# A fused linear-attention and MLP kernel: the hand-written order of its work, the priorities of its kinds of instruction and two buffer counts are changed

## The chip, the cores and the metric

The kernel runs on one core of a Trainium2 chip. The metric is the device time in microseconds (us) of one execution, the median of three runs. TensorE is called PE here, its weight loads PEld, VectorE DVE, ScalarE ACT, GpSimd POOL; SyncE (SP) issues all DMAs.

## The reference

```python
B, H, S, D = 4, 8, 768, 48
mag = sqrt(a_re**2 + a_im**2); scale = minimum(mag, 0.999) / (mag + 1e-6)
ar, ai = a_re * scale, a_im * scale
for t in range(S):                       # a complex decay per channel, one state per head
    S_re, S_im = ar*S_re - ai*S_im + outer(k[t], v[t]), ar*S_im + ai*S_re
    y[t] = q[t] @ S_re
x = y as (B*S, H*D) = (3072, 384)
h = x @ w_in                             # (3072, 2048)
out = (h - tanh(h)) @ w_out              # (3072, 384)
```

The inputs a, q, k, v are float32 and the weights reach the kernel as 64-bit words.

## The kernel before

The recurrence is computed in 6 chunks of 128 time steps (`NC`), for 4 batches; a *unit* u is one chunk of one batch (24 of them), a *pair* g is two units of one chunk (12 of them). Every product that needs more than 16 bits is made of three passes over a high and a low float16 half (`PASS`). The first four units (`PLAIN`) use float32 matmuls instead.

The work of a pair is cut into steps that a plan names by letters:

- `F`, `B`, `b`, `C`, `D`, `E`: the gates of a pair (L236 to L328). B and b take logarithms and exponentials of the decay, C the arctangent and the running sums of the angles (two matmuls with `tri` per batch, `cumsum`, L215) after loading the `carry` of the chunk before, D the sines (`g_trig`), E the running sums of the logarithms and their exponentials (`g_ep`, `g_en`), and `hd` by a trip through DRAM. `F0` and `F1` are the first pair's.
- `p`: `products(u)` (L371), in three pieces: q times its gates, split in two halves and transposed by a DMA into `qT` (L405); k the same into `kT`; then v and the load of the unit two further on.
- `a`: `attention(u)` (L428), in five pieces: S for four heads (12 matmuls of `kT` with `qT`, L450), masked on DVE into `af`; S for the other four heads; QU, the old state's part (L467, 24 matmuls of `qT` with `z16`); AV (L474), which ends with y scaled into `x16` and transposed by a DMA into `xT` (L479) and a square for a later check (`junk`, L480); Z, the new state. A sixth call does nothing.
- `i`, `o`: `decode` (L172) of two of the 16 tiles of w_in or w_out into two float16 halves, only before and during pair 0; `q` loads q, k, v of a unit; `w`: a square of decoded weights for the check (L198).

The main loop (L604 to L620) runs over the 12 pairs, and in each over 8 values of fp: `head(g, fp)` (L507) makes 18 matmuls of `xT` with w_in into `h`, then tanh on ACT and a subtraction on DVE (`mt`); after every second one `split` (L528) makes the two halves of g (`mg`); `tail` (L537) makes 12 matmuls into `o`, running up to LAG behind. Between them the steps of the plan are written down: a plan entry `5:a2` means: at step 5 (of 16, two for each fp; the even one after the head, the odd one after the tail), the next piece of attention of unit 2g+2. So while pair g goes through the MLP, the attention of pair g+1 is made. START holds for the time before pair 0, FIRST for pair 0, SECOND for pair 1, CYCLE for all others.

This is the order in the program. The order on each engine is laid down once, when the kernel is built, by a list scheduler with its own estimates of durations: of the instructions that it takes to be ready, the one that stands earliest in the program goes first, after its place has been moved forward by the offset of its kind (`At`, L93): OFFSET for pairs from 2 on, EARLY before that (L606). A negative offset moves it back. On the chip each engine works through its list in order and waits where an operand or a buffer is late. Activations that need a table are chained in program order by hand (`chained`, L335). DMAs are all in SP's list.

PSUM: three buffers for `h` (`ps_h`), three for `att` (`ps_a`: S, y, the running sums and the state's update share them), one pair for `o`. BUFS counts the buffers of some SBUF tiles; those without a count have one (`a_raw`, `g_t1`, `junk`).

Of the kernel before, what the change touches and what calls it, by code (L numbers as in the profile page):

```python
# [18 lines left out]
B, H, S, D = 4, 8, 768, 48  # L19
# [23 lines left out]
BUFS = {"io": 3, "wtmp": 4, "mt": 2, "mg": 4, "qkf": 2, "xT": 2, "a16": 3, "af": 2, "x16": 1, "qT": 4, "kT": 2, "vv": 2, "z16": 2}  # L43
LAG = 3
START = (
    "F0 F1 i0 B1 b1 i1 o3 q0 q1 p0 p0 i2 p1 p0 a0 p1 p1 o1 a1 o0 a0 a1 i5 E1 a1 i4 a1 a0 o4 C1 i3 i7 D1 a0 p2 "
).split()
FIRST = tuple((int(i), x) for i, x in (y.split(":") for y in (
    "0:p3 0:a0 0:a1 1:p2 1:i6 1:p2 2:a2 3:o7 3:o5 4:a2 4:a2 4:p3 5:B2 5:o2 5:b2 6:p3 7:a2 7:C2 9:a3 9:a2 9:a3 10:a3 11:D2 12:B3 12:b3 13:a3 14:E2 14:p4 14:p4 14:p4 15:o6 15:p5 15:a3 "
).split()))  # L50
SECOND = tuple((int(i), x) for i, x in (y.split(":") for y in (
    "0:p2 0:p2 1:a1 1:p2 2:a2 2:a2 3:C2 4:p2 4:p3 6:D2 7:p2 7:a2 7:a0 7:p3 7:a1 8:a2 9:a3 9:p2 9:w0 10:a3 10:a2 11:a3 11:E2 11:p4 11:B3 11:b3 13:a3 13:a3 14:w1 "
).split()))
CYCLE = tuple((int(i), x) for i, x in (y.split(":") for y in (
    "0:p2 0:p2 0:p3 0:w0 2:p2 2:p3 4:p3 4:a2 5:C2 5:a2 5:D2 7:a2 7:a2 8:a3 9:a3 9:a3 10:a2 10:a3 10:a3 10:B3 11:E2 11:b3 11:a2 15:w1 "
).split()))
OFFSET = {"gate": 2000, "gatep": -300, "prod": 0, "prodp": 400, "qkhi": 400, "vhi": -100, "vlo": -100, "zhi": -300, "zlo": -300, "S": 30, "af": -300, "ahi": 0, "alo": -2000, "qu": 0, "y": 0, "xf": 100, "kv": 30, "z": 30, "guard": -2000, "h": 0, "tanh": -30, "mt": 400, "ghi": 2000, "glo": 4000, "o": 0, "out": -30, "dec": -100, "dechi": 400, "declo": 4000, "table": 0, "cum": 0, "load": 2000}
EARLY = {"gate": 200, "gatep": 100, "prod": 0, "prodp": 2000, "qkhi": -30, "vhi": 0, "vlo": 700, "zhi": 4000, "zlo": -300, "S": 100, "af": 400, "ahi": -30, "alo": -100, "qu": 100, "y": 400, "xf": 0, "kv": 700, "z": 200, "guard": -30, "h": 0, "tanh": 30, "mt": -30, "ghi": 100, "glo": 4000, "o": 0, "out": -700, "dec": 0, "dechi": 1000, "declo": 400, "table": -300, "cum": 100, "load": 0}
# [28 lines left out]
def tile_fast(ctx: ExitStack, tc: tile.TileContext, flag, a_in, qkv_in, win_in, wout_in, sq_c, vec_c, lim_c, out):  # L87
# [84 lines left out]
    def decode(fp, kind):  # L172
        src = (win_in, wout_in)[kind]
        raw = sb.tile([P, 4, DM], F32, name="io", bufs=BUFS["io"]).rearrange("p x n -> p (x n)").bitcast(I32).rearrange("p (n two) -> p n two", two=2)
        for j in range(2):
# [650 lines left out]
```

## Time and profile before

| what | value |
|---|---|
| time before, median of 3 runs | 584.81 us (583.1 to 588.11) |
| the profiled execution | 584.0 us |
| its span, first to last instruction | 582.2 us |
| busy: PE, PEld, DVE, ACT | 506.6, 386.9, 459.2, 452.5 us |
| mean granted TensorE clock | 0.967 |

The difference between the profiled execution and its span, 1.8 us, lies around the program. A stretch of the span is read by setting its length against the busy time of each engine in it: an engine that is busy throughout sets its length. Matmuls are pipelined, so that the row of one overlaps the start of the next by up to 0.2 us.

### The profile page before, as it was taken

The numbers are of one execution on the slowest core, as the hardware profiler recorded it, in microseconds if no ns is written. First come the engines' busy times: TensorE is split into PE (matmuls) and PEld (weight loads), VectorE is DVE, ScalarE is ACT, GpSimd is POOL, SyncE is SP. The second block draws the span as 40 slices with busy tenths as digits, with TensorE's granted clock in tenths as the row PEclk, the third lists the DMA queues.
The fourth block names the chain that finished last, engine by engine and source line by source line (L and its number), as shares of the span: only waits on it lengthen the run. The fifth ranks groups of instructions, "written<-read, shape, count | busy, mean of one in ns | idle before, by whom it ended". The sixth has DMA issues, their size and how long they took to land.

```text
span 582.2 us, 12341 instructions
## 1 busy us (share of the span) xinstructions
PE 506.6 (87%) x5058; PEld 386.9 (66%) x5058; DVE 459.2 (79%) x674; ACT 452.5 (78%) x784; POOL 1.9 (0%) x8
## 2 busy tenths in 40 slices
PE   2564989978999889889889989889889899999995
PEld 0343867756678668668668668668668577787772
DVE  4999998876998978878978977977987977953321
ACT  7988899978888968968968968968978969643441
POOL 1000000000000000000000000000000000000000
PEclk9886899988999999999999999999999899999998
DMA  8778632096473573583763572762672641720001
GB/s 259 237 254 224 212 126 78 16 186 137 79 163 98 101 141 97 101 142 97 101 140 97 108 137 94 109 142 87 120 155 65 138 103 49 139 69 15 1 28 33
DMA packets 133899, 68.07 MB, mean 117 GB/s; under 512 B 119982, under 2 KB 123694, under 8 KB 133836
## 3 DMA queue, kind: packets, MB, share of 16 engines
q1 hardware_dynamic: 133836, 67.21, 49.9%
q8 instruction: 41, 0.67, 0.5%
q14 instruction: 22, 0.18, 0.1%
HBM read 36.73 MB, written 4.78 MB: 71 GB/s over the span
## 4 chain that ended last, share of the span: by engine, by line
PE 47%; DVE 17%; ACT 14%; DMA 13%; issue 6%; SPq 1%; ACTq 0%; DVEq 0%
PE h L515 16%; PE o L546 16%; PE att L102 11%; DMA kT<-k 6%; DMA qT<-q 3%; DVE g_t L102 3%; DVE a_raw L102 2%; ACT a_raw L102 2%; DVE qkv_raw L390 2%; PE att L467 2%; DMA g_t<-carry 2%; DVE qkf L393 2%; ACT L346 2%; DVE k L119 2%; ACT g_t L102 1%
## 5 line engine op out<-in xcount | busy, mean ns | idle before, releaser
L515 PE MATMUL h<-xT,w 128*128 128x256 f16 x1728 | 212.8, 275 | 18.6 <-DMA xT<-x 16.5
L546 PE MATMUL o<-w,mg 128*128 128x384 f16 x1152 | 207.8, 327 | 1.4 <-DVE mg L102 1.3
L515 PEld LDWEIGHTS <-w 128*128 128x128 f16 x1728 | 168.0, 99 | 48.8 <-issue 11.9
L546 PEld LDWEIGHTS <-mg 128*128 128x128 f16 x1152 | 111.6, 98 | 66.7 <-DVE mg L102 2.0
L102 ACT ACTIVATE mt<-h 128x512 f32<-128x512 f32 x96 | 56.4, 590 | 56.8 <-PE h L515 56.5
L102 DVE SCALAR_TENSOR_TENSOR mt<-h,mt 128x512 f32<-128x512 f32 x96 | 65.3, 685 | 38.9 <-ACT mt L102 38.9
L102 DVE SCALAR_TENSOR_TENSOR mg<-mt,mg 128x1024 f16<-128x1024 f32 x48 | 58.7, 1222 | 21.8 <-ACT mg L102 21.4
L102 PE MATMUL att<-qT,kT 96*128 96x128 f16 (+1 forms) x544 | 46.9, 236 | 16.9 <-DMA kT<-k 14.1
L102 ACT ACTIVATE mg<-mt 128x1024 f16<-128x1024 f32 x48 | 50.5, 1052 | 7.7 <-DVE mt L102 7.5
L102 ACT ACTIVATE a_raw<-a_raw 128x768 f32<-128x768 f32 (+2 forms) x49 | 39.2, 802 | 6.3 <-DVE a_raw L102 6.1
L102 PEld LDWEIGHTS <-kT 96*128 96x128 f16 x480 | 30.9, 101 | 18.6 <-DMA kT<-k 17.1
L393 DVE TENSOR_TENSOR qkf<-qkv_raw,g_trig 128x768 f32<-128x768 f32 x44 | 40.9, 949 | 0.0
L102 DVE TENSOR_TENSOR af<-att,sqc 128x512 f32<-128x512 f32 x40 | 27.4, 688 | 14.9 <-PE att L102 14.7
L346 ACT ACT_TABLE_LOAD x24 | 30.8, 1283 | 0.4
L102 DVE TENSOR_TENSOR a<-af,a 128x512 f16<-128x512 f32 x40 | 26.8, 684 | 2.9 <-ACT a L112 2.9
L102 ACT ACTIVATE q<-qkf 128x768 f16<-128x768 f32 x20 | 16.9, 844 | 10.4 <-DMA qT<-q 10.4
L112 ACT ACTIVATE a<-af 128x512 f16<-128x512 f32 x36 | 21.7, 626 | 2.9 <-DVE af L102 2.9
L102 DVE SCALAR_TENSOR_TENSOR g_t<-g_t,a_raw 128x768 f32<-128x768 f32 (+1 forms) x26 | 23.0, 887 | 0.9 <-ACT a_raw L102 0.9
L102 ACT ACTIVATE g_t<-att 128x384 f32<-128x384 f32 x24 | 10.7, 485 | 15.7 <-PE att L221 9.9
L102 ACT ACTIVATE g_trig<-g_t 128x768 f32<-128x768 f32 (+1 forms) x26 | 20.3, 782 | 0.3 <-DVE g_t L102 0.2
L102 ACT ACT_TABLE_LOAD x15 | 19.2, 1283 | 1.0 <-PEq L819 0.8
L119 DVE TENSOR_TENSOR q<-qkf,q 128x768 f16<-128x768 f32 x20 | 19.0, 950 | 1.2 <-ACT q L102 1.2
(96 smaller groups left out, 674.4 us busy)
## 6 DMA issues: line engine op xcount, KB each, us to landing
qkv_raw<-in_qkv SPq DMA_DIRECT2D x24, 576.0 KB
a_raw<-in_a SPq DMA_DIRECT2D x22, 384.0 KB
io<-in_win SPq DMA_DIRECT2D x16, 384.0 KB
io<-in_wout SPq DMA_DIRECT2D x16, 384.0 KB
out_dram<-io SPq DMA_DIRECT2D x24, 192.0 KB
a_raw<-in_a SPq DMA_DIRECT2D x4, 192.0 KB
xT<-x SPq DMA_TRANSPOSE x24
hd<-hscr SPq DMA_DIRECT2D x20, 3.0 KB
```

The costliest lines, as they stand in the source:

```text
L102: return f(*a, **k)
L112: A(kind).activation(out=out, in_=in_, func=AF.Copy, scale=scale)
L119: by_name[ENGINE[which]](kind).tensor_tensor(**k)
L346: chained(A("table").preload_act_table_set(name))
L390: V("prod").scalar_tensor_tensor(out=x, in0=vw(e), scalar=E_MAX, in1=x, op0=ALU.min, op1=ALU.mult)
L393: V("prod").tensor_tensor(out=f, in0=x[:, :, None].broadcast_to([P, H, 2, D]), in1=tg[:, :, sl].rearrange("p r (h d) -> p h r d", d=D), op ...
L467: T("qu").matmul(y_ps[:, h * D:(h + 1) * D], lhsT=qT[0:K, qp * H + h], rhs=z16[0:K, zp, h * D:(h + 1) * D], start=(h == 0 and n == 0), sto ...
L515: T("h").matmul(h_ps[:, j].rearrange("p (two t) -> p two t", two=2), lhsT=wi[ft][:, wp, kt * P:(kt + 1) * P], rhs=xT[:, :, xp, kt, :], sta ...
L546: T("o").matmul(o_ps[:, tt, :DM], lhsT=gg[:, gp, fp % 2, j * 256 + tt * P:j * 256 + (tt + 1) * P], rhs=wo[ft][:, wp], start=(ft == 0 and n ...
```

## The change

Two buffer counts, the three plans and START, and offsets of some kinds are other numbers or another order; no function changes. `qux` and `prodp` are not used by any function. In CYCLE the order of the pieces of attention of unit 2g+3 goes from steps 8, 9, 9, 10, 10 to 7, 9, 10, 10, 10, and the second product of that unit from step 2 to 1; C2 and D2 stand together; w0 and w1 go from steps 0 and 15 to 3 and 13.

```diff
--- before.py
+++ after.py
@@ -40,23 +40,23 @@
 STEP = [round((s + 1) * DEC / math.log(2)) for s in range(P)]
 PLAIN = 4
 HALF = [n // 2 for n in STEP]
-BUFS = {"io": 3, "wtmp": 4, "mt": 2, "mg": 4, "qkf": 2, "xT": 2, "a16": 3, "af": 2, "x16": 1, "qT": 4, "kT": 2, "vv": 2, "z16": 2}
+BUFS = {"io": 3, "wtmp": 4, "mt": 2, "mg": 3, "qkf": 2, "xT": 2, "a16": 3, "af": 2, "x16": 1, "qT": 3, "kT": 2, "vv": 2, "z16": 2}
 LAG = 3
 START = (
-    "F0 F1 i0 B1 b1 i1 o3 q0 q1 p0 p0 i2 p1 p0 a0 p1 p1 o1 a1 o0 a0 a1 i5 E1 a1 i4 a1 a0 o4 C1 i3 i7 D1 a0 p2 "
+    "F0 i0 o3 F1 B1 i1 q0 q1 p0 p0 i2 p1 p0 a0 p1 b1 o0 p1 a1 o1 a0 a1 i5 E1 a1 i4 a1 i3 a0 o4 C1 i7 a0 D1 p2 "
 ).split()
 FIRST = tuple((int(i), x) for i, x in (y.split(":") for y in (
-    "0:p3 0:a0 0:a1 1:p2 1:i6 1:p2 2:a2 3:o7 3:o5 4:a2 4:a2 4:p3 5:B2 5:o2 5:b2 6:p3 7:a2 7:C2 9:a3 9:a2 9:a3 10:a3 11:D2 12:B3 12:b3 13:a3 14:E2 14:p4 14:p4 14:p4 15:o6 15:p5 15:a3 "
+    "0:p3 0:a0 0:a1 1:p2 1:i6 1:p2 2:a2 3:o7 3:a2 3:o5 3:a2 4:p3 4:B2 5:b2 6:p3 7:a2 7:C2 7:o2 9:a3 9:a2 9:a3 10:D2 10:a3 12:B3 12:b3 13:a3 13:a3 14:E2 14:p4 14:p4 15:o6 15:p5 "
 ).split()))
 SECOND = tuple((int(i), x) for i, x in (y.split(":") for y in (
-    "0:p2 0:p2 1:a1 1:p2 2:a2 2:a2 3:C2 4:p2 4:p3 6:D2 7:p2 7:a2 7:a0 7:p3 7:a1 8:a2 9:a3 9:p2 9:w0 10:a3 10:a2 11:a3 11:E2 11:p4 11:B3 11:b3 13:a3 13:a3 14:w1 "
+    "0:p2 0:p2 0:a2 1:p2 2:p2 3:a2 3:C2 4:p2 5:a1 5:a1 5:p3 5:p2 6:D2 7:a2 8:p3 8:a2 9:a3 10:a3 10:p2 10:a2 11:a3 11:E2 11:p4 11:B3 11:b3 12:w0 13:a0 13:a3 14:a3 15:w1 "
 ).split()))
 CYCLE = tuple((int(i), x) for i, x in (y.split(":") for y in (
-    "0:p2 0:p2 0:p3 0:w0 2:p2 2:p3 4:p3 4:a2 5:C2 5:a2 5:D2 7:a2 7:a2 8:a3 9:a3 9:a3 10:a2 10:a3 10:a3 10:B3 11:E2 11:b3 11:a2 15:w1 "
+    "0:p2 0:p2 0:p3 1:p3 1:a0 2:p2 3:w0 4:a2 4:p3 5:C2 5:D2 5:a2 7:a2 7:a2 7:a3 9:a3 10:a2 10:a3 10:a3 10:a3 10:B3 11:E2 11:b3 13:w1 "
 ).split()))
-OFFSET = {"gate": 2000, "gatep": -300, "prod": 0, "prodp": 400, "qkhi": 400, "vhi": -100, "vlo": -100, "zhi": -300, "zlo": -300, "S": 30, "af": -300, "ahi": 0, "alo": -2000, "qu": 0, "y": 0, "xf": 100, "kv": 30, "z": 30, "guard": -2000, "h": 0, "tanh": -30, "mt": 400, "ghi": 2000, "glo": 4000, "o": 0, "out": -30, "dec": -100, "dechi": 400, "declo": 4000, "table": 0, "cum": 0, "load": 2000}
-EARLY = {"gate": 200, "gatep": 100, "prod": 0, "prodp": 2000, "qkhi": -30, "vhi": 0, "vlo": 700, "zhi": 4000, "zlo": -300, "S": 100, "af": 400, "ahi": -30, "alo": -100, "qu": 100, "y": 400, "xf": 0, "kv": 700, "z": 200, "guard": -30, "h": 0, "tanh": 30, "mt": -30, "ghi": 100, "glo": 4000, "o": 0, "out": -700, "dec": 0, "dechi": 1000, "declo": 400, "table": -300, "cum": 100, "load": 0}
-ENGINE = {"qhi": "A", "khi": "A", "qlo": "V", "klo": "V", "cos": "V", "sin": "V", "zhi": "A", "qux": "V", "zmul": "V", "xf0": "V", "tr": "A", "vd": "A", "lsb0": "V", "lsb1": "V", "base": "A", "dechi": "A", "declo": "V", "abs": "A", "thhi": "A", "t2hi": "A", "t2lo": "V", "xhi": "A", "xlo": "V", "vhi": "A", "ahi": "A", "alo": "V", "ghi": "A", "glo": "V", "nf": "A", "t1": "V"}
+OFFSET = {"gate": 2000, "gatep": -300, "prod": 0, "prodp": 0, "qkhi": 400, "vhi": -100, "vlo": -100, "zhi": -300, "zlo": -30, "S": 30, "af": 0, "ahi": 0, "alo": -2000, "qu": 700, "y": 0, "xf": 100, "kv": 30, "z": -30, "guard": -100, "h": 0, "tanh": -30, "mt": 400, "ghi": 2000, "glo": 4000, "o": 0, "out": 4000, "dec": 2000, "dechi": 400, "declo": 4000, "table": 0, "cum": 0, "load": 2000}
+EARLY = {"gate": 200, "gatep": 100, "prod": 0, "prodp": 200, "qkhi": -30, "vhi": 0, "vlo": 2000, "zhi": 4000, "zlo": -300, "S": 100, "af": 400, "ahi": 200, "alo": -100, "qu": 4000, "y": 400, "xf": 0, "kv": 700, "z": 200, "guard": -30, "h": 0, "tanh": 30, "mt": -30, "ghi": 100, "glo": 700, "o": 0, "out": -700, "dec": 0, "dechi": 1000, "declo": 400, "table": -300, "cum": 0, "load": 0}
+ENGINE = {"qhi": "A", "khi": "A", "qlo": "V", "klo": "V", "cos": "V", "sin": "V", "zhi": "A", "qux": "A", "zmul": "V", "xf0": "V", "tr": "A", "vd": "A", "lsb0": "V", "lsb1": "V", "base": "A", "dechi": "A", "declo": "V", "abs": "A", "thhi": "A", "t2hi": "A", "t2lo": "V", "xhi": "A", "xlo": "V", "vhi": "A", "ahi": "A", "alo": "V", "ghi": "A", "glo": "V", "nf": "A", "t1": "V"}
 TABLES = {
     AF.Ln: ("natural_log_exp_and_others",),
     AF.Exp: ("natural_log_exp_and_others", "exp_and_others"),
```

## Rows read from the trace of the kernel before

**Rows 1.** The page, its first part: busy us of each engine (share) xinstructions
```profile
PE 506.6 (87%) x5058; PEld 386.9 (66%) x5058; DVE 459.2 (79%) x674; ACT 452.5 (78%) x784; POOL 1.9 (0%) x8
```

**Rows 2.** Stretches cut at each pair's first head: length, busy us (instructions) by engine, granted clock
```profile
0.00:57.80 57.80, 25.93 (x113) 18.24 (x114) 48.06 (x70) 49.20 (x90) 1.94 (x8) 0.86 0.80 245
57.80:108.20 50.40, 46.36 (x373) 37.26 (x374) 48.16 (x70) 46.62 (x74) 0.00 (x0) 0.96 0.40 126
108.20:161.80 53.60, 46.28 (x458) 34.02 (x457) 43.60 (x63) 44.33 (x78) 0.00 (x0) 0.90 0.57 113
...
201.00:244.90 43.90, 39.49 (x441) 30.48 (x442) 36.23 (x55) 35.77 (x64) 0.00 (x0) 1.00 0.56 113
...
417.10:460.30 43.20, 38.47 (x434) 29.80 (x435) 36.86 (x55) 36.21 (x65) 0.00 (x0) 1.00 0.55 119
```

**Rows 3.** What PE waited for, 201 to 461 us: total us, times, longest
```profile
PE h L515 <- DMA xT<-x: 12.4, 7, 2.7
PE att L102 <- DMA kT<-k: 7.9, 6, 1.7
PE att L221 <- ACT a_raw L102: 5.1, 5, 1.4
```

**Rows 4.** The chain that ended last, 280 to 340 us: start, us, what
```profile
286.22 6.21 DMA qT<-q
...
294.57 0.82 ACT junk L102 x2
```

**Rows 5.** PE in order of time in one pair: start, us, instruction, [idle before it]
```profile
290.40 2.13 PE L515 MATMUL h<-xT,w 128*128 128x256 f16 x18
...
294.04 0.84 PE L102 MATMUL att<-qT,kT 96*128 96x128 f16 x12 [1.35 <-DMA kT<-k]
...
298.48 2.11 PE L546 MATMUL o<-w,mg 128*128 128x384 f16 x12
...
304.42 0.48 PE L221 MATMUL att<-a_raw,tri 128*128 128x384 f16 x2 [1.21 <-ACT a_raw L102]
304.74 0.83 PE L102 MATMUL att<-qT,kT 96*128 96x128 f16 x12
...
307.04 0.77 PE L467 MATMUL att<-z,qT 96*128 96x48 f16 x24
```

**Rows 6.** ACT, DVE and SP at the start of that pair, the same view
```profile
292.51 0.84 ACT L102 ACTIVATE q<-qkf 128x768 f16<-128x768 f32 x1 [2.47 <-DMA qT<-q]
...
294.47 0.83 ACT L102 ACTIVATE junk<-w 128x768 f16<-128x768 f16 x1
...
295.29 0.58 ACT L102 ACTIVATE mt<-h 128x512 f32<-128x512 f32 x1
295.50 1.81 SPq L405 DMA_TRANSPOSE qT<-q  x1
...
295.91 0.69 DVE L102 SCALAR_TENSOR_TENSOR mt<-h,mt 128x512 f32<-128x512 f32 x1 [0.48 <-ACT mt L102]
```

**Rows 7.** ACT later in that pair, the same view: x and the squares that release y
```profile
314.15 0.57 ACT L102 ACTIVATE junk<-att,vec 128x384 f16<-128x384 f32 x1
...
324.89 0.58 ACT L102 ACTIVATE x<-att,vec 128x384 f16<-128x384 f32 x1
...
332.01 0.58 ACT L102 ACTIVATE junk<-att,vec 128x384 f16<-128x384 f32 x1
```

**Rows 8.** PE in pair 1 and at the first head, and a stretch of pair 1
```profile
51.38 2.21 PE L102 MATMUL att<-af,a 128*128 128x48 f32 x16
57.75 0.61 PE L515 MATMUL h<-xT,w 128*128 128x256 f16 x2 [4.16 <-DMA xT<-x]
...
127.72 2.74 PE L102 MATMUL att<-qT,kT 96*128 96x128 f16 x24 [3.29 <-DMA kT<-k]
...
127.70:134.00 6.30, 6.28 (x39) 4.81 (x40) 1.84 (x3) 1.22 (x2) 0.00 (x0) 0.50 0.75 169
```

## The prediction

> **What bounds the kernel now.** I read the page first. PE is busy for 506.6 of 582.2 us [rows 1], far ahead of DVE and ACT, so a new order can only win PE's idle time. The table of stretches, cut where each pair's first `head` matmul starts, shows where that is [rows 2]. The reader should compare the stretch's length with PE's busy time. Before the first head, 25.93 of 57.80 us are busy. In pair 0 it is 46.36 of 50.40, but DVE is busy for 48.16 there, so that stretch belongs to DVE. Pair 1 has 46.28 of 53.60. Pairs 3 to 8, six of them, stand between the two shown, 39.49 of 43.90 (the first) and 38.47 of 43.20 (the last): 4.4 to 4.7 us idle in each of these two.
>
> The list of what PE waited for, cut to pairs 3 to 8, names three waits and no other [rows 3]: the first `head` of a pair waits for the transposed x (12.4 us, 7 times), the first S matmul for the transposed k (7.9 us, 6 times), the first running sum of the angles for its operand on ACT (5.1 us, 5 times); 25.4 us together. One pair, from 288.1 us, stands for the six.
>
> The chain of work that ended last [rows 4] tells what hangs together in such a pair: the transpose of q (6.21 us from issue to landing), two squares of weights on ACT (`junk`, 0.82 us on the chain), then the carry's load and the running sum. The engines' order of time in that pair gives the rest [rows 5 to 7].
>
> **What cannot change.** Every activation that needs a table is chained in program order (L335 to L346). B2 moves from step 5 to 4, D2 of the first plan from 11 to 10, and D2 of the cycle past a piece of attention; none of them passes another gate step or a tanh. So the sequence of tables, loads included, is the same, and the backbone of ACT with it. The sixth pieces of attention and surplus pieces of products that appear or vanish in the plans do nothing, as their generators have ended. `prodp` and `qux` have no user; `OFFSET["dec"]` has none either, as decodes stand only in START and FIRST, where EARLY holds. These cost nothing.
>
> **Buffers.** `mg` from 4 to 3: with LAG = 3, at most three tiles of g have tails left when a new one is written, so the third buffer is enough in program order; the last tail of the oldest is written down before the two heads that precede the new tile. If PE ran heads further ahead, a split of g would wait; with 12 `o` between heads in the trace [rows 5] it does not. `qT` from 4 to 3: a unit's buffer is then that of the unit three back, whose last reader was in the pair before. I take 0 for both; if I am wrong about `mg`, a wait like those of 1.2 to 1.4 us in [rows 5] comes once a pair, and C below would have it.
>
> **START, FIRST, SECOND.** i0 and o3 come ahead of F1, b1 behind the first products, i3 and i7 ahead of two pieces of a0, its AV ahead of D1. The same decodes and gates have to pass DVE before pair 0 ends, and DVE is busy for 48.06 and 48.16 us of 57.80 and 50.40 [rows 2]. What could be won is the 4.16 us for which the first head waits for x [rows 8]: there 16 of the y matmuls come only at 51.38. `cum` losing its 100 and AV standing ahead of D1 both help. But what starts sooner runs into DVE in pair 0. The gain is between 0 and 4.2 us, and a loss of the same size is as easy to make by a decode that gets ahead of the chain to x. On SP the loads of i0 and o3 stand ahead of F1's load of the next gates' input, but that load waits for its only buffer, which F0 and F1 still read, so it is not put back. I take 0. Moving two pieces of a2 from step 4 to 3, o2 from 5 to 7, the last a3 from 15 to 13 and the third p4 into the next plan all fall under the same cover, DVE in pair 0.
>
> **Guards at -100 instead of -2000, w0 and w1 at steps 3 and 13.** In the pair shown ACT idles for 2.47 us until the q transpose lands, then runs q, a tanh, k and only then a square of weights (294.47), and the tanh that DVE needs starts behind it at 295.29; DVE sits idle for 0.48 us until it ends [rows 6]. The low part of k, the split of g and the carry's load stand behind that on DVE and SP, and the running sum behind the load. With the square earlier, the idle 2.47 us cover it (0.83 us) and the chain is 0.48 us shorter. Bounds: 0 if the square stays there, 1.2 (the whole wait of the running sum [rows 5]) if more moves up. I take the 0.48 in each of the five pairs that have this wait: **-2.4 us**. The same edit frees the bank of y sooner: now the square that releases it runs at 314.15, and for the second unit at 332.01, 6.5 us after its x is done (324.89 + 0.58) [rows 7].
>
> **QU at 700 (4000 in the early plans), z lo at -30.** These 24 matmuls need the transposed q and z, not the transposed k. Now they run at 307.04 for 0.77 us, of which the last 0.16 overlap what follows (304.42 + 0.48 against 304.74), so they take 0.6 [rows 5]. In the pair shown q lands at 292.4 (286.22 + 6.21 [rows 4]), just before ACT's q starts at 292.51 [rows 6], and PE has already been brought to a stop before the S matmul that starts at 294.04, after 1.35 us of waiting for k. If the 24 stand just ahead of that S, they fill 0.6 us of each such wait: six pairs, **-3.6 us**. In pair 1 the wait for k is 3.29 us [rows 8] and two units have such matmuls; with the clock at 0.50 in the stretch behind it [rows 8], 0.6 to 0.8 us each, I take **-1.2 us** together. The other end: if they stand ahead of the head at 290.40, PE stops there until 292.4, 2.0 us instead of 1.35; that is a loss of 0.6 a pair. I take the first end, since in the row PE stood at S with q landed.
>
> **af at 0 instead of -300.** The mask multiply of the S that ended at 294.88 can run sooner on DVE; it has the size of the tanh's subtraction (128x512, 0.69 us [rows 6]). It frees a bank and starts the chain to y. PE waits for none of it in [rows 3]: 0, down to -0.3 a pair. **a3's first piece at 7, its QU at 10, p3's second at 1, out at 4000, z at -30**: `out` is one copy a pair and PE does not wait for it in [rows 3], nor for z; a3's pieces stand where PE is dense [rows 5]. The x of a3 is made at 324.89 [rows 7], in the backbone's own stretch of ACT (E2 follows in the plan), so an earlier S brings x no forward. 0.
>
> **Sum.** -2.4 - 3.6 - 1.2 = -7.2 us. The profiled execution took 584.0 us (span 582.2), so it would take 576.8. The median of the runs is 584.8, 0.8 above it; on its scale I forecast **577.6 us**.
>
> **Rivals.**
> B, *the waits only move*: the order was laid down with transposes that land sooner than they do. PE came to S 1.35 us before k landed; if QU is laid down as much too early against q, PE waits those 1.35 us at QU instead, the S behind it no longer waits, and nothing is won but the guards' 2.4 us (what queues behind it is the second head, and ACT's tanh behind that), which a gain or loss in the start (up to 4.2) can hide. For it: the transposes of q and k land one after the other, so one error holds for both. Time: 584.8 - 2.4 = 582.4, between 579 and 590. The change would do what it says in the program and not on the chip.
>
> C, *the banks run out* (slower): `att` has three banks. QU opens y's bank. Now it is opened at 307.04 and used up within some 7 us; opened where q lands, near 292.5, the first unit holds it for 15 us more, and the second, whose q is issued at 295.50 [rows 6], also. One bank is then left for S, two running sums, S again. Now the second S starts at 304.74, between two running sums [rows 5]; with one bank it must wait until DVE has read the first. That is 0.48 us of matmuls and then about 0.7 on DVE, by the 128x512 form; I count 0.8 of it as not covered by `o`. With QU's wait in front (0.6) it is 1.4 us in each of six pairs, 8.4, and 1 to 4 in pair 1, where a stop also halves the clock: 584.8 + 10 = **595 us**. It decides from the point where both y banks are open while the first running sum waits. Against it: the guards give y's bank back up to 6.5 us sooner, and `af` that of S.
> The Trainium skill ("Perfetto Trace Analysis", Optimization Strategy) says that a gap which keeps returning on the engine that should be saturated can mean too little SBUF or PSUM for the next tile. In before, the rows name transposes and an ACT result for the returning gaps, not a bank [rows 3], so the trace does not bear that out for the old order; by that rule the new one, which holds banks longer, would go as C.
>
> **How the numbers follow.** About 1% is what a measurement of this kernel can tell from no change: 579.0 to 590.7. I give the forecast 0.42, B 0.32, C 0.26. The forecast's own range is 568 to 579: its lower end has the k and running-sum waits gone altogether (7.9 + 5.1) and pair 1's 3.3 with them, 584.8 - 16.3. The range over all cases goes from there to 597, two above C's centre; what I leave out is a start that gains its 4.2 as well and a C to which a wait for `mg` is added.
>
> **What would show it.** In the profile after, PE's list of waits in pairs 3 to 8 should have k below 5 us and the running sum below 3, with x where it was; the 24 QU matmuls just ahead of the first S of the pair; no square of weights between k's copy and the tanh. B shows as a PE wait for q of about the size that k's was. C shows as PE waits at S or the running sums for DVE `af` or `g_t`, and longer pairs. If the time differs in the first 160 us and the pairs are as before, the step at fault is my 0 for the start.

## The result

The median of 12 runs went from 584.48 us (582.25 to 588.11) to 580.55 us (577.09 to 582.71). The ratio is 0.9923, with a 95% interval from 0.9896 to 0.995: 4.5 us less, between 2.9 and 6.1 (the two medians alone differ by 3.9). The forecast was 7.2 less.

The profiled execution of after took 582.7 us with a span of 580.9; that of before took 584.0 with 582.2. So the two spans stand only 1.3 us apart. The table of stretches shows why. First the busy time of each engine, from the page of after:

```profile
PE 512.5 (88%) x5058; PEld 391.5 (67%) x5058; DVE 458.6 (79%) x674; ACT 453.6 (78%) x784; POOL 1.9 (0%) x8
```

PE's is 5.9 us more than in [rows 1], 5.0 of them before the first head (30.91 against 25.93), where the granted clock was lower.

Stretches of after, cut like those of before at each pair's first head: length, then busy us (instructions) of PE, PEld, DVE, ACT and POOL, granted clock, DMA share, GB/s. The first three rows answer to the first three of [rows 2], the fourth is pair 2; the row from 201.40 to 458.40 is the six pairs 3 to 8 together.

```profile
0.00:60.90 60.90, 30.91 (x113) 22.45 (x113) 48.02 (x70) 49.71 (x90) 1.94 (x8) 0.79 0.76 232
60.90:110.30 49.40, 46.13 (x360) 37.47 (x361) 45.71 (x66) 45.43 (x72) 0.00 (x0) 0.91 0.43 128
110.30:158.50 48.20, 42.63 (x448) 32.16 (x446) 42.83 (x65) 43.68 (x77) 0.00 (x0) 0.96 0.54 113
158.50:201.40 42.90, 40.23 (x445) 30.79 (x445) 38.76 (x59) 37.50 (x64) 0.00 (x0) 1.00 0.54 119
...
201.40:458.40 257.00, 237.53 (x2634) 182.12 (x2634) 217.61 (x326) 214.16 (x379) 0.00 (x0) 1.00 0.59 116
458.40:580.90 122.50, 115.07 (x1062) 86.55 (x1062) 65.64 (x94) 63.07 (x107) 0.00 (x0) 0.98 0.27 60
```

The same large stretches of before, for comparison (pairs 0 to 2; pairs 3 to 8; what follows took 121.9 us):

```profile
57.80:201.10 143.30, 130.28 (x1251) 100.58 (x1252) 127.50 (x188) 126.19 (x211) 0.00 (x0) 0.95 0.49 118
201.10:460.40 259.30, 235.66 (x2635) 181.86 (x2636) 217.78 (x326) 214.13 (x379) 0.00 (x0) 1.00 0.55 115
```

Pairs 0 to 2 take 49.4 + 48.2 + 42.9 = 140.5 instead of 143.3 us (-2.8). Pairs 3 to 8 take 257.0 instead of 259.3 (-2.3). The end takes 0.6 more. Together that is -4.5 us. That it equals the measured gain is partly chance, as the stretches of single executions vary too (table below). The time before the first head is 3.1 us longer (60.9 against 57.8), but one execution can't put that down to the change: in before and in five experiments below that leave this time as it was (e1, e2, e3, e5, e11) it is 57.8, 59.0, 59.5, 60.7, 62.2 and 58.3 us, with the same instructions in the same order on PE, DVE and ACT. A single span carries this spread of 4.4 us; the median of many runs evens it out. The seven kernels with the start of after lie between 60.0 and 62.4, 61.0 on average against 59.6, so that a start about 1.5 us longer is not excluded.

Most of the gain of pairs 0 to 2 lies in pair 1. There PE's wait for k, in before and then in after (total us, times, longest), is

```profile
PE att L102 <- DMA kT<-k: 6.2, 3, 3.3
PE att L102 <- DMA kT<-k: 4.2, 2, 3.1
```

The third of these waits has moved into pair 2, where it is 0.6 us. Behind the waits the granted clock was 0.50 for 6.83 us from 127.15 [rows 8] and for another 3.41 us in before, and once in after:

```profile
144.22:147.63 3.41, 3.41 (x60) 3.00 (x56) 3.10 (x5) 1.55 (x6) 0.00 (x0) 0.50 0.00 0
131.41:134.82 3.41, 3.41 (x27) 2.72 (x25) 2.08 (x3) 1.12 (x2) 0.00 (x0) 0.50 0.72 151
```

Half clock costs at most half of its time: 5.1 us in before and 1.7 in after. With the 2.0 us of waits that would be the whole 5.4 us by which pair 1 is shorter. A part of it belongs to the one execution: in the other five kernels with the start of before, pair 1 has 6.83 us at half clock; of the seven with that of after, five have 3.41, one (e6) none and one (e9) 6.83.

What PE waited for in pairs 3 to 8 of after (total us, times, longest):

```profile
PE h L515 <- DMA xT<-x: 5.8, 6, 1.8
PE att L102 <- DMA kT<-k: 4.6, 4, 1.3
PE att L474 <- DVE a L102: 3.2, 6, 0.5
PE att L221 <- ACT a_raw L102: 2.9, 4, 1.2
PE att L102 <- ACT k L102: 1.7, 1, 1.7
PE att L102 <- ACT mt L102: 0.9, 1, 0.9
```

The window of [rows 3] holds seven first heads; cut to six, x in before is 9.7 us:

```profile
PE h L515 <- DMA xT<-x: 9.7, 6, 2.1
PE att L102 <- DMA kT<-k: 7.9, 6, 1.7
PE att L221 <- ACT a_raw L102: 5.1, 5, 1.4
```

So 22.7 us of named waits became 19.1. That is more than the 2.3 us by which these pairs are shorter; PE's busy time for the same matmuls rose by 1.9 (235.66 to 237.53, both at clock 1.00). A stop that is shorter than the overlap of two rows (up to 0.2 us) counts as busy here. The waits for x and for the running sum shrank. The wait for k did not go away: the last two rows of after belong to the same S matmul in the two pairs in which k is missing from the list, and 4.6 + 1.7 + 0.9 = 7.2 stands against 7.9. A new wait appears, 0.5 us in each pair, where AV (L474) waits for the masked S on DVE.

One pair of after, from 286.9 us, in PE's order of time; it answers to [rows 5]:

```profile
292.80 0.84 PE L102 MATMUL att<-qT,kT 96*128 96x128 f16 x12 [1.35 <-DMA kT<-k]
...
301.15 1.46 PE L546 MATMUL o<-w,mg 128*128 128x384 f16 x8
303.09 0.48 PE L221 MATMUL att<-a_raw,tri 128*128 128x384 f16 x2 [0.48 <-ACT a_raw L102]
303.41 0.83 PE L102 MATMUL att<-qT,kT 96*128 96x128 f16 x12
...
305.03 0.77 PE L102 MATMUL att<-z,qT 96*128 96x48 f16 x24
...
316.50 0.42 PE L474 MATMUL att<-vv,a 128*128 128x48 f16 x10 [0.54 <-DVE a L102]
```

The first S still waits 1.35 us for k, and QU (`att<-z,qT`, 305.03) still stands behind the second S and the running sums, not ahead of the first S. What changed ahead of the running sum is its cover: 8 `o` run there, where before has 4 (row at e1), and the wait is 0.48; in before it was 1.21.

ACT in that pair, which answers to [rows 6]:

```profile
287.43 0.85 ACT L102 ACTIVATE junk<-w 128x768 f16<-128x768 f16 x1
...
291.07 0.84 ACT L102 ACTIVATE q<-qkf 128x768 f16<-128x768 f32 x1 [1.76 <-DMA qT<-q]
291.82 0.83 ACT L102 ACTIVATE k<-qkf 128x768 f16<-128x768 f32 x1
292.56 1.06 ACT L102 ACTIVATE mt<-h 128x512 f32<-128x512 f32 x2
293.51 0.84 ACT L102 ACTIVATE junk<-w 128x768 f16<-128x768 f16 x1
```

One square of weights now runs before the wait for q, and the other behind the two tanhs: none stands any more between k's copy and the tanh. That part happened as forecast.

### The profile page after: what moved, and what is told of

It is laid out like the page before. It is cut to its first block, busy times and chain, and to the rows that moved or that the text cites. A ratio compares the mean times of both kernels' runs of the same rounds, so it can differ in the third digit from the quotient of the medians.

```text
span 580.9 us, 12346 instructions
## 1 busy us (share of the span) xinstructions
PE 512.5 (88%) x5058; PEld 391.5 (67%) x5058; DVE 458.6 (79%) x674; ACT 453.6 (78%) x784; POOL 1.9 (0%) x8
## 4 chain that ended last, share of the span: by engine, by line
PE 48%; DVE 18%; ACT 15%; DMA 10%; issue 6%; SPq 1%; ACTq 0%; DVEq 0%
PE h L515 17%; PE o L546 15%; PE att L102 12%; DMA kT<-k 5%; DVE g_t L102 3%; ACT a_raw L102 2%; DVE a_raw L102 2%; DMA qT<-q 2%; DVE qkf L393 2%; DVE qkv_raw L390 2%; ACT L346 2%; DMA g_t<-carry 2%; ACT g_t L102 2%; DVE mt L102 2%; PE att L221 1%
## 5 line engine op out<-in xcount | busy, mean ns | idle before, releaser
L515 PE MATMUL h<-xT,w 128*128 128x256 f16 x1728 | 214.8, 276 | 14.9 <-DMA xT<-x 12.8
L546 PE MATMUL o<-w,mg 128*128 128x384 f16 x1152 | 210.2, 327 | 0.6 <-DVE mg L102 0.6
L515 PEld LDWEIGHTS <-w 128*128 128x128 f16 x1728 | 169.3, 99 | 47.4 <-issue 11.3
L102 ACT ACTIVATE mt<-h 128x512 f32<-128x512 f32 x96 | 55.8, 591 | 51.6 <-PE h L515 51.4
L102 DVE SCALAR_TENSOR_TENSOR mt<-h,mt 128x512 f32<-128x512 f32 x96 | 64.9, 685 | 31.8 <-ACT mt L102 31.8
L102 DVE SCALAR_TENSOR_TENSOR mg<-mt,mg 128x1024 f16<-128x1024 f32 x48 | 58.7, 1222 | 18.2 <-ACT mg L102 17.8
L102 PE MATMUL att<-qT,kT 96*128 96x128 f16 (+1 forms) x544 | 45.6, 233 | 14.7 <-DMA kT<-k 9.3
L102 ACT ACTIVATE mg<-mt 128x1024 f16<-128x1024 f32 x48 | 50.5, 1052 | 8.0 <-DVE mt L102 7.8
L102 ACT ACTIVATE a_raw<-a_raw 128x768 f32<-128x768 f32 (+2 forms) x49 | 39.2, 801 | 12.9 <-DVE a_raw L102 12.8
L102 PEld LDWEIGHTS <-kT 96*128 96x128 f16 x480 | 29.9, 99 | 16.4 <-DMA kT<-k 14.9
L452 DVE TENSOR_TENSOR af<-att,sqc 128x512 f32<-128x512 f32 x36 | 24.7, 687 | 8.0 <-PE att L102 8.0
L102 DVE TENSOR_TENSOR a<-af,a 128x512 f16<-128x512 f32 x40 | 27.1, 682 | 1.5 <-ACT a L112 1.5
L102 DVE SCALAR_TENSOR_TENSOR g_t<-g_t,a_raw 128x768 f32<-128x768 f32 (+1 forms) x26 | 23.0, 889 | 0.7 <-ACT a_raw L102 0.7
L119 DVE TENSOR_TENSOR q<-qkf,q 128x768 f16<-128x768 f32 x20 | 19.1, 953 | 4.7 <-ACT q L102 4.6
L102 ACT ACTIVATE q<-qkf 128x768 f16<-128x768 f32 x20 | 16.9, 845 | 6.6 <-DMA qT<-q 5.6
L102 ACT ACTIVATE g_t<-att 128x384 f32<-128x384 f32 x24 | 10.7, 486 | 12.7 <-PE att L221 12.2
L102 ACT ACTIVATE g_trig<-g_t 128x768 f32<-128x768 f32 (+1 forms) x26 | 20.3, 781 | 0.1
```

The lines of the kernel that those rows point to most:

```text
L102: return f(*a, **k)
L119: by_name[ENGINE[which]](kind).tensor_tensor(**k)
L452: V("af").tensor_tensor(out=af.rearrange("p (j t) -> p j t", j=4), in0=s_ps.rearrange("p (j t) -> p j t", j=4), in1=(causal if plain else ...
L515: T("h").matmul(h_ps[:, j].rearrange("p (two t) -> p two t", two=2), lhsT=wi[ft][:, wp, kt * P:(kt + 1) * P], rhs=xT[:, :, xp, kt, :], sta ...
L546: T("o").matmul(o_ps[:, tt, :DM], lhsT=gg[:, gp, fp % 2, j * 256 + tt * P:j * 256 + (tt + 1) * P], rhs=wo[ft][:, wp], start=(ft == 0 and n ...
```

## The experiments

Each kernel was run beside runs of before on the same chip. "Ratio" is its time to theirs, with the 95% interval. The stretches are those of each one's profiled execution: to the first head; pairs 0 to 2; pairs 3 to 8; the rest. "PE waits" are the named waits in pairs 3 to 8, in us.

| kernel | ratio | stretches, us | PE waits, pairs 3 to 8 |
|---|---|---|---|
| before | 1 | 57.8, 143.3, 259.3, 121.9 | x 9.7, k 7.9, running sum 5.1 |
| after | 0.9923 [0.9896, 0.995] | 60.9, 140.5, 257.0, 122.5 | x 5.8, S 7.2, AV 3.2, running sum 2.9 |
| e1 before, `af` | 0.9964 [0.9935, 0.9993] | 59.0, 143.6, 256.5, 121.6 | x 9.0, k 7.9, running sum 2.7 |
| e2 before, guards | 0.9989 [0.9954, 1.0025] | 59.5, 143.4, 256.8, 121.8 | x 9.3, S 7.1, running sum 3.7 |
| e3 before, QU | 1.0143 [1.0084, 1.0202] | 60.7, 144.0, 263.2, 123.4 | x 9.4, S 8.1, running sum 4.1, bank 1.8 |
| e11 before, QU and guards | 1.0048 [1.0023, 1.0074] | 58.3, 142.2, 260.0, 122.9 | x 5.0, S 8.2, running sum 3.4, AV 2.1 |
| e4 before, start | 0.9972 [0.994, 1.0004] | 60.8, 138.7, 261.9, 122.7 | x 9.6, k 7.7, running sum 5.9 |
| e12 before, EARLY alone | 0.9996 [0.9976, 1.0017] | 60.6, 141.9, 260.2, 121.5 | |
| e5 before, steady pairs | 1.0006 [0.9969, 1.0044] | 62.2, 146.4, 257.2, 121.2 | |
| e6 after, QU written first | 1.0116 [1.007, 1.0161] | 62.4, 139.2, 265.2, 124.9 | x 8.6, q 6.6, running sum 6.0, k 0.5 |
| e7 the same, QU at 0 | 1.0117 [1.0063, 1.017] | 60.9, 140.5, 265.3, 123.0 | running sum 13.1, x 8.3 |
| e8 after, x sooner | 1.0095 [1.006, 1.0129] | 62.2, 137.1, 265.7, 123.7 | k 11.4, running sum 6.8, AV 1.3 |
| e10 after, QU back | 0.9931 [0.9895, 0.9967] | 60.1, 135.7, 257.0, 125.1 | running sum 10.3, S 6.1 |
| e9 before, start, `af`, guards | 0.9898 [0.9868, 0.9928] | 60.0, 140.2, 254.5, 120.2 | x 8.7, S 6.9, running sum 1.5 |

"S" adds the rows whose wait ends the first S, whatever they name.

### e1: before with the mask multiply sooner

```diff
 OFFSET
-"af": -300
+"af": 0
```

> The kernel before with one number changed, af at 0 instead of -300 from pair 2 on. The prediction on record gave this edit 0 (down to -0.3 us a pair). Second theory, from the two traces: the mask multiply done sooner lets 8 instead of 4 matmuls o stand ahead of the first running sum, which in the profile after waits 0.48 us instead of 1.21; four o are 4 x 0.162 = 0.65 us, in five or six pairs 3.2 to 3.9 us, so 581 us where before has 584.5. A new wait of the y matmuls for DVE (0.5 us a pair in the profile after) may take it back; then 584.

0.9964 [0.9935, 0.9993], about 2.1 us faster, with pairs 3 to 8 shorter by 2.8 in its profile. The forecast had 0 for this edit, since PE waits for no mask multiply in [rows 3]. PE in the same pair of this kernel:

```profile
302.52 1.46 PE L546 MATMUL o<-w,mg 128*128 128x384 f16 x8
304.33 0.48 PE L221 MATMUL att<-a_raw,tri 128*128 128x384 f16 x2 [0.35 <-ACT a_raw L102]
```

and in before, ahead of the running sum of [rows 5]:

```profile
302.39 0.81 PE L546 MATMUL o<-w,mg 128*128 128x384 f16 x4
```

There are 8 `o` between the last head and the running sum, in before 4. The wait falls from 1.21 to 0.35 us; over the six pairs from 5.1 to 2.7. The k wait stays at 7.9. So moving DVE's multiply moved four of PE's matmuls, in the laid-down order, to a place where PE had been idle. The gain is not in what waits for the multiply.

### e2: before with the squares sooner

```diff
 OFFSET
-"guard": -2000
+"guard": -100
```

> The kernel before with one number changed, guard at -100 instead of -2000 from pair 2 on. The prediction on record gives -2.4 us (0.48 us in each of five pairs, at the running sum): 582.1 us, and a running-sum wait of about 0.7 us instead of 1.2. Second theory: the squares of weights stand in ACT's slack either way, the order of PE moves by a few entries only; 584.5 within 1 us.

0.9989 [0.9954, 1.0025]: 0.6 us faster, with an interval from 2.7 faster to 1.5 slower. In its profile pairs 3 to 8 are 2.5 us shorter, very near the forecast 2.4. DVE's list of waits in these pairs shows that the step itself was right, in this kernel:

```profile
DVE mt L102 <- ACT mt L102: 3.0, 6, 1.3
```

and in before:

```profile
DVE mt L102 <- ACT mt L102: 9.9, 13, 2.2
```

DVE waits 6.9 us less for tanhs, yet PE's running-sum wait falls only from 5.1 to 3.7 and the S wait from 7.9 to 7.1. The runs neither show this gain nor exclude it. (The kind `guard` also holds the squares of the inputs, `rawsq`, which move with it.)

### e3 and e11: before with QU sooner, without and with the guards

```diff
 OFFSET
-"zlo": -300, "qu": 0
+"zlo": -30, "qu": 700
```

> The kernel before with two numbers changed, qu at 700 instead of 0 and zlo at -30 instead of -300 from pair 2 on. The prediction on record gives -3.6 us: 580.9, with the wait for k shorter by 0.6 us in six pairs. Second theory: in the profile after the 24 matmuls still stand behind the second S (305.03), so they fill no wait for k; that wait stays at 0.6 to 1.7 us and the time at 584.5 within 1 us.

1.0143 [1.0084, 1.0202]: the edit on which half of the forecast rested costs 8 us by itself. The list of PE's waits in pairs 3 to 8 has a row that before does not have:

```profile
PE att L102 <- ACT junk L102: 1.8, 6, 0.3
```

PE in one of these pairs, where it stands:

```profile
317.75 0.18 PE L102 MATMUL att<-vv,k 128*128 128x48 f16 x1 [0.31 <-ACT junk L102]
```

and ACT at the same time:

```profile
317.04 0.57 ACT L102 ACTIVATE junk<-att,vec 128x384 f16<-128x384 f32 x1
```

The second unit's QU runs sooner, ahead of the first unit's state update (`att<-vv,k`). The update then waits for the square, y's last reader, so it must have got the bank of y. (Which bank a matmul writes is read from such waits; the rows leave buffer numbers out.) This is rival C's mechanism, `att` banks running out, though at the state update and not at the second S where C put it. The Trainium skill ("Perfetto Trace Analysis", Optimization Strategy) says that a gap which keeps returning on the engine that should be saturated can mean too little SBUF or PSUM for the next tile; here the trace agrees, once in each of six pairs, 0.3 us each. The 1.8 us of this row are not the whole loss of 3.9 in these pairs. Most of the rest stands in PE's busy time, 238.8 instead of 235.7 us for the same matmuls at clock 1.00, that is in stops too short for a row. QU has such stops: in the pair shown DVE's mask multiplies, which read S, end at 310.80 and 314.16 us, and the two QU start at 310.85 and 314.21, so QU waits there for a bank that S held. Rival C had put such a wait at S, not at QU.

If the square's release of the bank is the cause, the same edit together with the guards must lose less than the two apart.

```diff
 OFFSET
-"zlo": -300, "qu": 0, "guard": -2000
+"zlo": -30, "qu": 700, "guard": -100
```

> The kernel before with qu at 700, zlo at -30 and guard at -100 from pair 2 on. QU alone lost 1.4%, and its profile shows a new PE wait for a square on ACT (6 times, 0.3 us and a little more, at the first matmul of the state's update) and pairs 0.7 us longer. If a bank of y held until that square is the cause: that wait is gone, pairs 3 to 8 are back at 259 us or under it, ratio 0.997 to 1.002. If QU's place itself is the cause: ratio 1.01 as alone.

1.0048 [1.0023, 1.0074], pairs 3 to 8 at 260.0 instead of 263.2. The row with `junk` is gone:

```profile
PE h L515 <- DMA xT<-x: 5.0, 6, 1.0
...
PE att L474 <- DVE a L102: 2.1, 6, 0.4
```

The guards are worth 1.0143 - 1.0048 = 0.95% where QU is early and 0.1% where it is not (e2). So they and QU hang together through the bank, as rival C's paragraph said they might ("the guards give y's bank back up to 6.5 us sooner"). Even so QU at 700 does not pay on the order of before. Here x's wait is short, as in after, and the AV wait for DVE is there too. On the order of before, neither QU nor the guards alone show either. Shorter waits for x did not make this kernel faster than before.

### e4, e12, e5: the start alone, its offsets alone, the steady pairs alone

e4 has START, FIRST, SECOND and EARLY of after and is otherwise before; e12 has only EARLY of after; e5 has only CYCLE, OFFSET and BUFS of after.

```diff
-START, FIRST, SECOND, EARLY of before
+START, FIRST, SECOND, EARLY of after
```

> The kernel before with START, FIRST, SECOND and EARLY of the changed kernel, and its own CYCLE, OFFSET and buffers. The prediction on record gives 0 for the start and -1.2 us for the QU matmuls in pair 1: 583.3. Second theory: the profiles reach the head of pair 3 at 201.0 us before and 201.4 after, with the first head 3.1 us later, pair 1 shorter by 5.4 and pair 2 longer by 3.7: 584.5 within 1 us. A rival: the start holds most of the 4 us gained, and the one profile after is of an execution 2 us slower than the median; then 581.

> The kernel before with EARLY of the changed kernel alone (START and the plans as before). PE's list of pair 1 then has the second unit's QU in one piece and the first S of pair 2 no longer in pair 1, as in the changed kernel, but still two heads in front of the first o. If the gain of 3.6 us in pairs 0 to 2 comes from priorities: pairs 0 to 2 at about 140 us, ratio 0.994. If from the plans: 143 us, ratio 1.000.

e4 gives 0.9972 [0.994, 1.0004], e12 0.9996 [0.9976, 1.0017]. Stretches of e4: pairs 0 to 2, and a piece of pair 8:

```profile
60.80:199.50 138.70, 126.77 (x1251) 99.10 (x1252) 126.38 (x187) 125.57 (x210) 0.00 (x0) 0.97 0.50 121
...
433.44:436.85 3.41, 3.41 (x26) 1.91 (x25) 2.28 (x4) 1.80 (x4) 0.00 (x0) 0.50 0.74 228
```

Pairs 0 to 2 are 4.6 us shorter than in before. Every kernel with the start of before has 142.2 us or more there (143.3, 143.6, 143.4, 144.0, 146.4, 142.2), every kernel with that of after 140.5 or less (140.5, 138.7, 139.2, 140.5, 137.1, 135.7, 140.2), and e12 141.9 between them. So the plans, alone or with EARLY, carry this gain; EARLY alone was not seen to. It shortens pairs 0 and 1 (99.7 us together, against 102.2 to 104.0 in the kernels with the start of before), but pair 2 takes 42.2 us then, against 39.2 in before. Which of the three plans gains was not tried, and the whole time of e4 is only 1.6 us less, not clear of the noise. The 261.9 us of pairs 3 to 8 are 2.6 more than in before, whose order they have. One pair, 46.4 us long, holds that: PE stopped for the running sum there and then ran at half clock (the second row above):

```profile
429.46 0.81 PE L546 MATMUL o<-w,mg 128*128 128x384 f16 x4
432.22 0.48 PE L221 MATMUL att<-a_raw,tri 128*128 128x384 f16 x2 [1.95 <-ACT a_raw L102]
```

```diff
-CYCLE, OFFSET, BUFS of before
+CYCLE, OFFSET, BUFS of after
```

> The kernel before with OFFSET, CYCLE and the buffer counts of the changed kernel, and its own START, FIRST, SECOND and EARLY. If the gain of the change (ratio 0.9923, 4.5 us) is made from pair 2 on, this has it whole: 580. The prediction on record gives -6.0 for this part: 578.5. If the start holds the gain: 584.5.

e5 gives 1.0006 [0.9969, 1.0044], though its pairs 3 to 8 took 257.2, as in after. Its pairs 0 to 2 (146.4) were the longest of all, and its start (62.2) the longest with the START of before. e4 and e5 together are the whole change, and 0.9972 x 1.0006 = 0.9978 is a smaller gain than its 0.9923. The intervals just allow for the difference; whether the two halves help each other stays open.

### e6 and e7: after with QU written ahead of S

The forecast meant QU to stand ahead of the first S. In after it does not. So it was written there, in the program, with QU's offset as in after (e6) and at 0 (e7):

```diff
+        if c > 0:
+            y_ps = ps_a.tile([P, 512], F32, name="att")
+            for h in range(H):
+                for n, (qp, zp) in enumerate(PASS):
+                    T("qu").matmul(y_ps[:, h * D:(h + 1) * D], lhsT=qT[0:K, qp * H + h], rhs=z16[0:K, zp, h * D:(h + 1) * D], start=(h == 0 and n == 0), stop=False)
...
-        y_ps = ps_a.tile([P, 512], F32, name="att")
-        if c > 0:
-            for h in range(H):
-                for n, (qp, zp) in enumerate(PASS):
...
+        if c == 0:
+            y_ps = ps_a.tile([P, 512], F32, name="att")
```

> The changed kernel with the 24 QU matmuls written into the first piece of attention, ahead of S, so that y's bank is asked for before S's. PE's list then has them inside the first head of a pair. It tests the price that the prediction gave to QU in front of S. If they fill the wait for k: -0.6 us a pair, 577. If they stand so early that PE waits for q instead, up to 2.0 us where k cost 1.35: +0.6 a pair in eight pairs, 585. If y's bank, held for 15 us longer, is what counts: 590 or more, with PE waiting at S or the running sums for DVE.

1.0116 [1.007, 1.0161]. The k wait is all but gone, and PE waits at QU instead:

```profile
PE att L102 <- DMA qT<-q: 6.6, 5, 2.4
...
PE att L102 <- ACT mg L102: 1.2, 1, 1.2
PE att L102 <- DMA kT<-k: 0.5, 1, 0.5
```

That is the other end of the forecast's bound, and rival B's mechanism: QU laid down too early against q. The 7.2 us at S became 6.6 + 1.2 at QU, in six pairs, and 0.5 at S. But pairs 3 to 8 are 8.2 us longer than in after, and the named waits only 3.8. PE's busy time is 3.6 us more (241.16 against 237.53, both at clock 1.00), in short stops again, and here they carry rival C's sign: in the pair from 290.68 us DVE's mask multiplies end at 310.86 and 312.48 us, and S starts at 310.92 and 312.53. So QU ahead of S paid both prices, q's wait and the banks.

> As the run before, but with qu at 0 from pair 2 on. PE's list has the first S of a pair behind a third head, 12 o and 18 h later than in the changed kernel (about 4 us), and QU around it. The wait for k should be gone (1.35 us in each of six pairs, so -5 to -8: 573 to 576) unless the work taken from behind it is missed later, at the running sums or at x: then 580.

1.0117 [1.0063, 1.017]. With QU at 0 most of it falls between S's matmuls, and neither q nor k is waited for (L517 is L515 of after):

```profile
PE att L221 <- ACT a_raw L102: 13.1, 6, 2.7
PE h L517 <- DMA xT<-x: 8.3, 6, 1.7
```

The wait for the running sum rises from 2.9 to 13.1 us. So a transpose that is no longer waited for buys nothing by itself: PE only comes sooner to the next operand, which is no sooner.

### e8: after with x sooner

```diff
 OFFSET
-"xf": 100
+"xf": 3000
```

> The changed kernel with xf at 3000 instead of 100 from pair 2 on: y of the second unit is scaled into x ahead of the logarithms and exponentials of the gates on ACT, so that the transposed x of the next pair lands earlier. In the profile after, y is done at 316.93 and x is made at 323.04, and the head waits for it 0.6 to 2.1 us, 7.9 us in pairs 3 to 8. If this wait hangs on x's place on ACT: -5 to -8, 573 to 576. If the wait is taken over by the gates, which then end later and with them q and k: 580 or more.

The wait for x, the largest in after under one name, is gone; the time is 1.0095 [1.006, 1.0129].

```profile
PE att L102 <- DMA kT<-k: 11.4, 6, 2.9
PE att L221 <- ACT a_raw L102: 6.8, 4, 3.2
```

k rises from 7.2 to 11.4 and the running sum from 2.9 to 6.8, while AV falls from 3.2 to 1.3: the named waits are 19.5 us, against 19.1 in after. So the waits only moved. Nearly all of the 8.7 us by which pairs 3 to 8 are longer stands in PE's busy time, 245.5 instead of 237.5 us for the same matmuls at a mean clock of 0.97:

```profile
199.30:465.00 265.70, 245.50 (x2643) 186.29 (x2640) 218.24 (x326) 213.45 (x379) 0.00 (x0) 0.97 0.52 112
```

The waits are longer one by one, and behind four of those for k the clock fell for 3.41 us (last section); half of that, four times, is 6.8 us.

### e10: after without its QU edit

```diff
 OFFSET
-"zlo": -30, "qu": 700
+"zlo": -300, "qu": 0
```

> The changed kernel with qu at 0 and zlo at -300 from pair 2 on, as before the change. PE's list then has the first S of a pair behind a third head as in the run that lost 1.2%, but the running sum behind 12 h instead of 17. If QU's priority is what the steady part gains by: slower than the changed kernel. If it costs there what it cost alone (1.4%): ratio 0.985. If the waits move as in that run, from k to the running sum: the k wait gone, the running-sum wait above 10 us in pairs 3 to 8, ratio 1.00 to 1.01.

0.9931 [0.9895, 0.9967], against 0.9923 for after: taking the QU edit out of the change changes nothing that can be measured. Its waits are elsewhere again: none for x, and

```profile
PE att L221 <- ACT a_raw L102: 10.3, 6, 2.5
```

The named waits of pairs 3 to 8 are 16.4 us, 2.7 less than in after. Behind three of those for the running sum the clock fell, for 3.41 us each, and the six pairs take the same 257.0.

### e9: the parts that seemed to pay, on before

START, FIRST, SECOND and EARLY of after, and in OFFSET only `af` and `guard`; CYCLE, BUFS and all other offsets are those of before.

```diff
 OFFSET
-"af": -300, "guard": -2000
+"af": 0, "guard": -100
-START, FIRST, SECOND, EARLY of before
+START, FIRST, SECOND, EARLY of after
```

> The kernel before with START, FIRST, SECOND and EARLY of the changed kernel, af at 0 and guard at -100, and without the rest (CYCLE, buffers, qu, zlo, z, out as before). First theory, QU earlier is worth something in the changed kernel: this is worse than it, ratio 0.995 or more. Second theory, the gain of the change comes from pairs 0 to 2 (143.3 us in the orders of before, 139.6 in those of after, over the profiles so far) and from af and the guards (2.5 us each alone in pairs 3 to 8): 3.6 + 2.5 to 4 us, ratio 0.988 to 0.990.

The medians are 577.10 and 583.56 us, the ratio 0.9898 [0.9868, 0.9928]: the fastest kernel tried. Its interval overlaps that of after, and the two were timed beside different runs of before, so that it is below after is likely but not shown. The parts multiplied, 0.9972 x 0.9964 x 0.9989 = 0.9925, lie inside its interval. Pairs 3 to 8 of this kernel, a row of its stretches:

```profile
200.20:454.70 254.50, 235.80 (x2635) 181.92 (x2636) 218.15 (x326) 213.71 (x381) 0.00 (x0) 1.00 0.58 117
```

Pairs 3 to 8 are 4.8 us shorter than in before, twice the gain of after, and PE's busy time is what it was (235.80 against 235.66). The wait for the running sum, 5.1 us in before, is 1.5 us and left in two pairs of six. x (8.7) and S (6.9) are nearly what they were.

## Why the prediction was right and where it was not

The direction was right and the size too large: -7.2 us forecast, -4.5 measured (2.9 to 6.1). That the sum came near is partly luck: its largest term failed, and terms that stood at 0 brought part of what it was meant to bring. The measured 580.55 us lies above the forecast's own range (568 to 579) and in rival B's (579 to 590), and B's 582.4 is nearer to it than the forecast's 577.6.

- **QU, -3.6 and -1.2: the step that failed.** It said that the 24 matmuls would stand just ahead of the first S and fill its wait for k. They stand behind the second S in e3 and in after, and the wait of S is 7.2 us in after against 7.9. (The row for k alone, 4.6, meets the sign "below 5" only because two of the six waits stand under other names.) A larger offset only sets what goes first among the instructions that the scheduler takes to be ready; I read the place from where the trace had idle time, which the scheduler's own durations need not have. Alone the edit cost 1.43% (e3); within the change, undoing it made no difference (e10). And the place that I had in mind is no gain either: there PE waited 6.6 us for q, and S for banks (e6). The working named that end of the bound ("a loss of 0.6 a pair") and I took the other. The -1.2 in pair 1 cannot be told apart from the plans that moved that pair.
- **Guards, -2.4: the mechanism was right, the size is open.** The square left its place between k's copy and the tanh, DVE's wait for tanhs fell by 6.9 us (e2), and the pairs of that profile are 2.5 shorter. The runs of e2 give 0.6, with 2.4 inside the interval; after without this edit was not run. The second thing that the step claimed, that y's bank comes free sooner, was seen: it is worth 0.95% where QU is early (e3, e11).
- **`af`, 0: mis-sized.** It is worth 2.1 us alone (0.4 to 3.8, e1), by way of four `o` that moved ahead of the running sum. In after the same 8 `o` stand there; after without this edit was not run. I asked who waits for the multiply and did not ask what the scheduler puts elsewhere on PE when it comes sooner. The fall of the running-sum wait to below 3 us, which I had named as the guards' sign, is therefore not theirs alone: 2.7 with `af`, 3.7 with the guards, 2.9 in after, 1.5 with both on before's cycle (e9).
- **Start, 0: under-sized, and its cover holds for pair 0 alone.** Pairs 0 to 2 are 2.8 us shorter in after and 4.6 in e4. The text let all of it fall under one cover, DVE in pair 0. There the cover became thinner: DVE has 66 instructions and 45.71 us now, 70 and 48.16 before, and pair 2 has 59 instead of 55 (188 - 70 - 63). Pair 0 went from 50.40 [rows 2] to 49.40, and the profile of after has a fall of the clock there that before's has not; between executions alike in this the difference is some 2 to 2.5 (last section), about what DVE lost. I took the plans' moves one by one as hidden under DVE and did not count what they take off DVE. Pair 1, from 53.60 to 48.20, is not under that cover: DVE is busy for 43.60 us of it [rows 2]. There the waits for k and the half clock behind them shrank (the result), a stop that the working had priced for QU and not for the plans. Pair 2 grew from 39.2 (201.0 - 161.8) to 42.9. That the plans gain in these ways is argued from these rows; no run shows one alone. The bound that I gave, up to 4.2, was for the first head's wait, which is another place.
- **Buffers, 0: right as far as seen.** No wait of a split for `mg` stands in after's lists. SP's list has a row that before's has not, `SPq L405 <- PE att L102`, 6.8 us in six pairs: the second unit's q transpose names a matmul of S. The issue of that transpose takes 2.9 to 3.6 us there, but as long in e2 and e11, which have four `qT`, so that a cost of it is not shown. Alone the buffers were not run.
- **x "where it was": wrong.** It fell from 9.7 to 5.8. On the order of before it took QU and guards together: in e11 it fell likewise (5.0), in e1, e2, e3 it did not (9.0 to 9.4). But in e10, which has no QU edit, it is gone, so what holds it in after is not settled. In neither after nor e11 did it shorten the pairs by as much.
- **Rivals.** B, that waits only move, describes what happened to everything aimed at a transpose: e6, e7, e8 and e10 each emptied one wait and filled another. C, that the banks run out, describes e3, with `junk` and S as the holders, and a part of e6. In after the row with `junk` is gone, as C's "against" supposed, and a short stop at QU is left: it starts at 305.03, the mask multiply ends at 304.98. So each rival held a part of the truth, and as far as the runs show the gain came from two parts that I had put at nothing (`af`, the plans), perhaps with the guards.

## What to carry to other kernels

In a software-pipelined loop, waits for operands made one iteration earlier form a ring: to start one operand sooner, or to fill one wait, moves PE sooner to the next late operand (e7: from k to the running sum; e8: from x to k). What shortened this loop was to put work that was there anyway in front of the operand that came late (e1) and, as far as profiles tell, to take work off the chain that makes it (e2); e9 has both. A sum of waits is not the whole price: stops too short for a row (e3, e6) and a clock that falls behind long ones (e8) stand in the busy time, so compare that too, for the same matmuls. When a change is a bundle of priorities, a term of zero for "nobody waits for it" is not safe: ask also which instructions of other engines change their place, and time the parts, because one of them can eat what the others bring (e3).

## What the runs showed of the hardware that I had not expected

- **The clock can fall behind a stop of about 2 us in an otherwise busy stretch.** In e4 PE was idle for 1.95 us before the running sum at 432.22, and from 433.44 the granted clock was 0.50 for 3.41 us (row at e4), that is 1.2 instead of 2.4 GHz; that pair took 46.4 us, the one before it 42.2. In e8 the same came behind four waits for k; one of them in PE's order of time:

```profile
296.27 1.07 PE L102 MATMUL att<-qT,kT 96*128 96x128 f16 x12 [2.00 <-DMA kT<-k]
297.13 3.44 PE L546 MATMUL o<-w,mg 128*128 128x384 f16 x11
```

  Eleven `o` took 3.44 us there, where 12 take 2.11 at full clock [rows 5]. In pairs 3 to 8 of all these kernels, the stop at the head of pair 9 left out, there were ten such falls, each at or just behind the end of a stop of 1.83 to 2.87 us; 17 other stops of 1.8 to 3.2 us had none, among them one of 2.06 in before. What decides between them was not settled. In pair 0 the case is cleaner: in every kernel PE stops once for 2.06 us there, at a head (`h`) that waits for DVE's `mt`. The rows of PE up to it are the same in all fourteen profiles. Behind it the clock fell for 3.41 us in seven of them, after's among them, and not in the other seven. With the start of before, pair 0 took 50.2 to 50.9 us without that fall (before, e1, e2, e11) and 51.5 to 51.6 with it (e3, e5), so it cost about 1 us as far as these profiles tell; with the start of after it took 47.7 to 48.3 without (e4, e7, e10) and 48.8 to 49.5 with it. In after no fall came in pairs 3 to 8. Where waits are gathered into one, this price of up to half of 3.41 us belongs in the sum; mine had it for pair 1 only.
- **The time to the first head varies by 4.4 us** (57.8 to 62.2) between executions whose instructions there are the same. The granted clock was 0.86 in before (57.8 us) and 0.80 in e5 (62.2), but 0.76 in e3 (60.7), so it does not decide alone. What makes the time vary was not tried.
